# The first four token tiles of a transformer block kernel: two queues for the first load, normalisation on VectorE in column parts, casts in halves, another order of the first matmuls

## The chip, the cores and the metric

The kernel runs on one core of a Trainium2 chip. The metric is device microseconds of one execution; the number given for the kernel before is the median of its runs. A profiled execution, with a record of every instruction, is what the views of the profile are taken from.

## What is computed

`x` is 2048 tokens of 576 values. One block adds local attention and a two-layer Mish network, both on the same normalised tokens:

```python
xn = (x - mean(x)) / sqrt(var(x) + 1e-5)          # over the 576 values of a token
q, k, v = split(xn @ wqkv)                         # 32 heads of 18
# each token attends to itself and to tokens 2, 4, ... 14 before it
o = softmax(q . k * 18**-0.5 over those 8) @ v
h = xn @ w1 + b1                                   # 4608 wide
out = x + o @ wo + (h * tanh(softplus(h))) @ w2
```

All of it is float32. For the matmuls on TensorE (PE) each operand is split into a high and a low part of a shorter type (`fp32r` in the rows): the high part is a cast, the low part the residual, and a product is the sum of high·high, high·low and low·high.

## The kernel before, in words

The tokens are taken in two halves of 1024 (`hf`), each in two blocks of 512 (`b`, TB), each of four tiles of 128 tokens (`jj`, JB). The QKV weights come in four groups of 432 columns (`g`), each of five row blocks of 128 (576 values padded to 640). One item `qkv_item(hf, g, b, jj)` multiplies one token tile by one weight group: 14 matmuls into one PSUM tile `pq`, with a list `seq` of triples (row block of the tokens, row block of the weights, high or low part of the weights). A list `plan` holds the items in an order written out by hand; other work is hung on its slots (`before`, `at`). Each engine takes its instructions in the order of the program, and waits for others by semaphores. DMAs are issued by SP's queue (`nc.sync`) in the program's order.

The first half begins with the items of weight group 0 on tiles 0 to 3, by `first_item(n)` (L1205); then come group 1 on the same tiles and so on. This is the part that the change touches.

- **Start** (L49 to L65): ScalarE (ACT) loads its function table at L49; GpSimd (POOL) builds the identity matrix; 30 transposes of it (L65) keep PE busy until data are there ("warm").
- **Loads** (L1106 to L1113, `load_x` L51): on SP's queue in this order: token tile 0 (`acc_0_0_0`, shown as acc), two row blocks of group 0's weights (`rq0`), token tile 1, the other three row blocks. The function `hold` (L1115) puts the loads of tiles 2 and 3 behind tile 0's statistics, and behind them the weights of group 1 and the rest.
- **Normalisation of a tile**: `ln_stats` on VectorE (DVE; two BATCH_NORM_STATS2 at L112, an aggregate at L113); `ln_root` (variance plus epsilon on DVE, L158; logarithm and exponential on ACT, L159 and L160); `ln_newton` (DVE: one Newton step for the root, L167 to L169, and mean·root with its sign changed, L170); `ln_norm` (ACT: one pass over 576 columns with scale and bias, L180; POOL: a copy of the last 64 columns beside them, L181, so that the fifth row block is full).
- **Transpose and split** (`ln_transpose` L184, `transpose_split` L67): POOL keeps the last columns for later (`rem`, L192); four transposes on PE into the PSUM tile `ta` (L75) and a fifth into `tb` (L76); ACT casts `ta` to the high parts `xt` in one pass of 512 columns (L81), DVE subtracts to the low parts (L82); ACT casts `tb` (L86), DVE subtracts for its upper 64 partitions (L87).
- **Group 0's weights** (`first_cast` L1176): ACT casts each row block to its high part (L1179), POOL subtracts to the low part (L1180). Later groups have their casts on ACT (L254) and their residuals on DVE (L255).
- **Order**: `prologue` (L1183) writes tile 0's chain and the start of tile 1's, with the five weight casts between. In the item of tile n, `mid` (L1208) is put in before matmul number 11, 8 or 4: it transposes tile n + 1 and prepares the tile after that.

In the item of tile 0 to 2, `seq` is: high·high of row blocks 0 to 3, two low weights, the low tokens of row blocks 0 to 3, two low weights, and the two products of the fifth row block. In tile 3's item it goes row block by row block.

Of the kernel before, what the change touches and what calls it, by code (L numbers as in the profile page):

```python
# [8 lines left out]
F32 = mybir.dt.float32  # L9
# [30 lines left out]
def block_kernel(ctx: ExitStack, tc: tile.TileContext, x, wq, wo, w1, b1, w2, mask, out):  # L40
# [7 lines left out]

    nc.scalar.preload_act_table_set("natural_log_exp_and_others")  # L49

    def load_x(hf, blocks=range(NB), jjs=range(JB)):  # L51
        tiles = []
        xv = x[hf * SH:(hf + 1) * SH, :].rearrange("(p j) d -> p j d", j=TJ)
        for b in blocks:
            for jj in jjs:
                t = sb.tile([P, D], F32, tag="acc", bufs=9, name=f"acc_{hf}_{b}_{jj}")
                nc.sync.dma_start(t, xv[:, b * JB + jj, :])
                tiles.append(t)
        return tiles
# [3 lines left out]
    warm = ps.tile([P, 512], F32, tag="h", bufs=4, name="warm")  # L63
    for k in range(30):
        nc.tensor.transpose(warm[:, (k % 4) * P:(k % 4 + 1) * P], ident, ident)  # L65

    def transpose_split(src, dst, col, extra=None, pair=False):  # L67
        n = next(tpn)
        if pair:
            ta, tb = (ps.tile([P, 512], F32, tag="out", bufs=4, name=f"tt{k}_{n}") for k in range(2))  # L70
        else:
            ta = ps.tile([P, 512], F32, tag="h", bufs=4, name=f"ta_{n}")
            tb = ps.tile([P, 512], F32, tag="h", bufs=4, name=f"tb_{n}")
        for k in range(KT):
            nc.tensor.transpose(ta[:, k * P:(k + 1) * P], src[:, k * P:(k + 1) * P], ident)  # L75
# [5 lines left out]
        nc.scalar.copy(hi, tav)  # L81
        nc.vector.tensor_sub(dst[:, 5:5 + KT, col:col + P], tav, hi.bitcast(F32))  # L82
        e = 1 if extra is None else 2
        hr = dst[:, KT:KT + 5 * e - 4:5, col:col + P]
        tbv = tb.rearrange("p (k t) -> p k t", k=KT)[:, 0:e]
        nc.scalar.copy(hr, tbv)  # L86
        nc.vector.tensor_sub(hr[64:P], tbv[64:P], hr[64:P].bitcast(F32))  # L87

# [73 lines left out]
    def ln_newton(n0):  # L162
        g = group[n0]
        k, rs, ve, y, nm = g["k"], *(g[w][:, 0:g["k"]] for w in ("rs", "ve", "y", "nm"))
        if k == 1:
            r, v, y, m = rs[:, 0], ve[:, 0], y[:, 0], nm[:, 0]
            nc.vector.tensor_scalar(y, r, r, v, op0=ALU.mult, op1=ALU.mult)  # L167
            nc.vector.tensor_scalar(y, y, -0.5, 1.5, op0=ALU.mult, op1=ALU.add)
            nc.vector.tensor_scalar(r, r, y, None, op0=ALU.mult)  # L169
            nc.vector.tensor_scalar(m, g["mv"][:, 0, 0:1], r, -1.0, op0=ALU.mult, op1=ALU.mult)  # L170
        else:
# [4 lines left out]
    def ln_norm(n):  # L176
        g = group[n]
        i = n - g["n0"]
        xn = sb.tile([P, 5 * P], F32, tag="xn", bufs=XNB, name=f"xn_0_{n}")
        nc.scalar.activation(xn[:, 0:D], accs[0][n], AF.Identity, bias=g["nm"][:, i, :], scale=g["rs"][:, i, :])  # L180
        nc.gpsimd.tensor_copy(xn[:, D:D + 64], xn[:, KT * P:D])  # L181
        xns[0, n] = xn

    def ln_transpose(hf, b, jj):  # L184
        if jj == 0:
# [7 lines left out]
        else:  # L193
            nc.gpsimd.tensor_tensor(out=rem, in0=rem, in1=xn[:, KT * P:], op=ALU.subtract)
        transpose_split(xn, XTs[hf, b], jj * P, rem if b else None, (hf, b) == (1, 0) and jj < 3)

# [130 lines left out]
    def qkv_item(hf, g, b, jj, mid=None, mid_at=4):  # L327
# [855 lines left out]
    def prologue():  # L1183
# [15 lines left out]
        ln_norm(1)  # L1199
        first_cast(4, nc.gpsimd)()  # L1200
        ln_stats(2)

    def first_item(n):
# [391 lines left out]
```

## Time and profile before

| | |
|---|---|
| Time before | 1114.05 us, median of 3 runs (1113.94 to 1114.44) |
| Profiled execution | 1114.25 us |
| Its span | 1112.5 us, 18203 instructions |
| Granted TensorE clock, mean | 1.00 |
| Busy, share of the span | PE 99%, PE weight load 91%, DVE 76%, POOL 71%, ACT 45% |
| Chain that ended last, by engine | PE 87%, POOL 6%, DVE 3%, issue 2%, ACT 1% |
| DMA | 271.60 MB, mean 244 GB/s |

Times are in microseconds unless marked ns. The span runs from the first to the last recorded instruction. PE is TensorE's matmul side, PEld its weight load, which overlaps PE; DVE, ACT, POOL and SP are VectorE, ScalarE, GpSimd and SyncE, and a name with q behind it (SPq) is that engine's queue. L12 is line 12 of the kernel. A row of the timeline gives start, busy time, engine, line, operation, out<-in, tile size, the count of instructions, and in brackets the idle time before it with what ended it. A row of the chain of waits gives start, length, and who held the chain. A row of the stretches gives the window, its length, then busy time with the count of instructions for PE, PEld, DVE, ACT and POOL, the granted clock, the DMA engines' busy share, and GB/s. A row of a line's instructions gives shortest, median and longest duration in ns, and between which times they ran. In a row of the costliest groups stand busy time and mean ns of one, then the idle time before them and what ended most of it.

### The profile page before, as it was taken

How to read it: one execution, taken by the hardware profiler on the slowest of the kernel's cores; microseconds unless marked ns; L12 is line 12 of the kernel's file. 1: busy time of each engine (PE TensorE's matmuls, PEld its weight loads, DVE VectorE, ACT ScalarE, POOL GpSimd, SP SyncE). 2: the span in 40 equal slices, each digit the busy share in tenths (PEclk: the TensorE clock that was granted, in tenths of full speed). 3: DMA queues.
4: the chain of work that ended last, by engine and by line, in shares of the span. 5: the costliest groups of instructions: out<-in, count | busy, mean ns of one | idle time of the engine just before them, and what ended most of it. 6: DMA issues, size and time to landing. Idle time of an engine off the chain costs nothing.

```text
span 1112.5 us, 18203 instructions
## 1 busy us (share of the span) xinstructions
PE 1101.6 (99%) x6550; PEld 1015.2 (91%) x6550; DVE 849.5 (76%) x1367; ACT 499.5 (45%) x917; POOL 790.8 (71%) x639
## 2 busy tenths in 40 slices
PE   9999999999999999999999999999999999999998
PEld 8999899999999999999999889989989999999998
DVE  6369788888889888897656577786776677777786
ACT  5544655544454544555333354433433344343353
POOL 2479777766679688785788676666688976867532
PEclk9999999999999999999999999999999999999999
DMA  6899696868777758675597898565664657776574
GB/s 202 283 312 316 225 356 214 285 233 276 258 242 264 268 208 301 249 249 204 190 323 241 245 375 307 211 196 196 220 222 170 209 195 223 244 288 219 171 232 142
DMA packets 178270, 271.60 MB, mean 244 GB/s; under 512 B 53218, under 2 KB 120068, under 8 KB 178180
## 3 DMA queue, kind: packets, MB, share of 16 engines
q1 hardware_dynamic: 178180, 270.44, 71.6%
q8 instruction: 52, 0.85, 0.3%
q14 instruction: 38, 0.31, 0.1%
HBM read 160.39 MB, written 110.00 MB: 243 GB/s over the span
## 4 chain that ended last, share of the span: by engine, by line
PE 87%; POOL 6%; DVE 3%; issue 2%; ACT 1%; DMA 0%; SPq 0%; POOLq 0%; DVEq 0%; ACTq 0%
PE h L669 28%; PE po L767 21%; PE pq L348 9%; PE po L880 9%; PE po L859 6%; PE h L675 5%; PE o L1063 5%; PE z L446 3%; POOL pv L571 2%; POOL accP L868 1%; POOL pr L533 1%; POOL act L721 1%; POOL s L620 1%; DMA acc<-in_x 0%; PE ta L75 0%
## 5 line engine op out<-in xcount | busy, mean ns | idle before, releaser
L767 PEld LDWEIGHTS po<-w,act 128*128 128x128 f32 x1728 | 236.4, 188 | 6.0 <-POOL act L721 0.4
L767 PE MATMUL po<-w,act 128*128 128x288 f32 x1728 | 240.7, 295 | 0.1
L533 POOL TENSOR_TENSOR pr<-q,kv 128x576 f32<-128x576 f32 x128 | 196.9, 1563 | 8.5 <-DMA q<-q_d 5.0
L721 POOL TENSOR_TENSOR act<-c,act 128x512 fp32r<-128x512 f32 x81 | 107.3, 1325 | 128.6 <-ACT act L720 128.6
L571 POOL TENSOR_TENSOR pv<-L,kv 128x576 f32<-128x576 f32 x128 | 177.9, 1484 | 26.1 <-DVE L L564 21.2
L771 DVE TENSOR_TENSOR acc<-po,acc 128x288 f32<-128x288 f32 x288 | 119.4, 448 | 29.9 <-PE po L767 29.0
L348 PE MATMUL pq<-wq,xt 128*128 128x432 f32 x672 | 136.5, 361 | 1.0 <-ACT xt L81 1.0
L880 PEld LDWEIGHTS po<-w,act 128*128 128x128 f32 x960 | 130.9, 188 | 4.6 <-DVE accP L883 1.8
L880 PE MATMUL po<-w,act 128*128 128x288 f32 x960 | 133.5, 295 | 1.0 <-DVE accP L883 1.0
L348 PEld LDWEIGHTS pq<-wq,xt 128*128 128x128 f32 x672 | 125.0, 188 | 8.0 <-ACT xt L81 1.8
L715 ACT ACTIVATE c<-c,b1c 128x512 f32<-128x512 f32 x81 | 58.7, 725 | 140.7 <-DVE c L714 140.4
L669 PE MATMUL h<-xt,t 128*128 128x512 f32 x432 | 110.6, 391 | 0.5 <-DVE rt L714 0.3
L669 PE MATMUL h<-S,t 128*128 128x512 f32 x432 | 110.5, 391 | 0.0
L577 DVE TENSOR_REDUCE og<-pv 128x144 f32<-128x1152 f32 x64 | 86.0, 1345 | 25.7 <-POOL pv L571 25.6
L669 PE MATMUL h<-xt,wa 128*128 128x512 f32 x432 | 104.1, 390 | 0.0
L538 DVE TENSOR_REDUCE L<-pr 128x64 f32<-128x1152 f32 x64 | 85.8, 1341 | 23.8 <-POOL pr L533 23.7
L703 ACT COPY c<-h 128x512 f32<-128x512 f32 x81 | 47.4, 586 | 124.1 <-PE h L675 73.0
L859 PEld LDWEIGHTS po<-pw,u 128*128 128x128 f32 x672 | 92.2, 188 | 5.4 <-DVE u L813 2.1
L859 PE MATMUL po<-pw,u 128*128 128x288 f32 x672 | 94.3, 295 | 2.5 <-DVE u L813 1.6
L669 PEld LDWEIGHTS h<-xt,wa 128*128 128x128 f32 x432 | 80.9, 188 | 17.0
L669 PEld LDWEIGHTS h<-xt,t 128*128 128x128 f32 x432 | 79.0, 188 | 15.7 <-DVE rt L714 0.7
L883 DVE TENSOR_TENSOR accP<-po,accP 128x288 f32<-128x288 f32 x160 | 68.9, 452 | 29.8 <-PE po L880 28.2
(228 smaller groups left out, 1853.8 us busy)
## 6 DMA issues: line engine op xcount, KB each, us to landing
kv<-kv_d SPq DMA_DIRECT2D x64, 396.0 KB, 5.1
kept_t<-t SPq DMA_DIRECT2D x36, 512.0 KB, 4.8
t<-kept_t SPq DMA_DIRECT2D x36, 512.0 KB, 6.7
rw<-in_w SPq DMA_DIRECT2D x36, 320.0 KB, 4.4
kept_wa<-wa SPq DMA_DIRECT2D x18, 640.0 KB, 4.7
kept_w<-w SPq DMA_DIRECT2D x20, 576.0 KB, 4.1
wa<-kept_wa SPq DMA_DIRECT2D x18, 640.0 KB, 5.2
w<-kept_w SPq DMA_DIRECT2D x20, 576.0 KB, 4.1
```

What stands on the lines that cost most here:

```text
L348: nc.tensor.matmul(pq[:, 0:432], XT[:, xi, tok], wt[wi][:, hl, 0:432], start=i == 0, stop=i == len(seq) - 1)
L533: nc.gpsimd.tensor_tensor(out=pr[:, x:x + hh], in0=q[:, j0 + x:j0 + x + hh, None, :].to_broadcast([P, hh, W, CU]), in1=win(kt, 0, CU, j0 + ...
L538: nc.vector.tensor_reduce(L[:, k, j0:j0 + hj].rearrange("p j w h -> p (j w h)"), pr.rearrange("p j w (h d) -> p (j w h) d", h=2), axis=AX, ...
L571: nc.gpsimd.tensor_tensor(out=pr[:, x:x + hj].rearrange("p j d w -> p j w d"), in0=L[:, k, x:x + hj, :, h:h + 1].to_broadcast([P, hj, W, DH]),
L577: nc.vector.tensor_reduce(og[:, c0:c0 + DH, :].rearrange("p d j -> p j d"), pr, axis=AX, op=ALU.add)
L669: nc.tensor.matmul(ph, wt[:, wl, wk * P:(wk + 1) * P], X[:, xs, :], start=first and i == 0, stop=last and i == len(seq) - 1, skip_group_ch ...
L721: nc.gpsimd.tensor_tensor(out=a[:, 1, :], in0=t, in1=a[:, 0, :].bitcast(F32), op=ALU.subtract)
L767: nc.tensor.matmul(po, acts[hf, q, b, j][:, al, tok], done["w2", hf, 2 * q + j][:, wl, c * HC:(c + 1) * HC], start=i == 0, stop=i == 5)
L771: nc.vector.tensor_tensor(out=t, in0=po, in1=t, op=ALU.add)
L859: nc.tensor.matmul(po, units[e, k, qq][:, al, tok], w[:, qq, wl, :], start=i == 0, stop=i == 5)
L880: nc.tensor.matmul(po, acts[hf, q, b, j][:, al, tok], done["w2", hf, 2 * q + j][:, wl, c * HC:(c + 1) * HC], start=i == 0, stop=i == 5)
L883: nc.vector.tensor_tensor(out=t, in0=po, in1=t, op=ALU.add)
```

## The change

The edits all lie in the first four token tiles, weight group 0:

- **First load**: tile 0 is loaded in two halves of 64 partitions, one issued by ACT's queue, one by SP's. ACT's function table is loaded behind that issue.
- **Warm-up**: 24 transposes instead of 30.
- **Normalisation** of tiles 0 to 3: DVE computes (x - mean)·root in three parts, columns 0 to 255, 256 to 575, and the last 64 again into the padding. ACT's pass, POOL's copy and the DVE instruction for the bias (L170) go, for these tiles.
- **Casts in halves**: for these tiles ACT casts `ta` in two passes of 256 columns (`apart`). In tile 0 the subtractions come in halves too; `transpose_split` hands the subtractions back as functions, so that the caller places them.
- **Order**: in the prologue the first two weight casts come behind tile 0's Newton step, the third and fourth around tile 1's statistics, the fifth behind tile 1's Newton step. In the items, `mid` comes before matmul number 11, 12 and 12: transposes of tile n + 1, then statistics and root of tile n + 2, then the subtractions of tile n + 1, then Newton and normalisation of tile n + 2. Tile 0's item has a `seq` of its own, written out; tiles 1 and 2 have all four low weights in a row.

In the changed kernel the lines are: load L56 to L59, warm-up L67, transposes L77 and L78, casts of `ta` in halves L90, subtractions L86 and L87 (tile 0: L94 by halves), cast of `tb` L92 (tile 0: L96), normalisation on DVE L194, weights' high and low parts L1198 and L1199, the items' matmuls L366, later weights' residuals L271.

```diff
...
-    nc.scalar.preload_act_table_set("natural_log_exp_and_others")
...
-                nc.sync.dma_start(t, xv[:, b * JB + jj, :])
+                if (hf, b, jj) == (0, 0, 0):
+                    nc.scalar.dma_start(t[64:P], xv[64:P, 0, :])
+                    nc.sync.dma_start(t[0:64], xv[0:64, 0, :])
+                else:
+                    nc.sync.dma_start(t, xv[:, b * JB + jj, :])
...
-    for k in range(30):
+    for k in range(24):
         nc.tensor.transpose(warm[:, (k % 4) * P:(k % 4 + 1) * P], ident, ident)
...
-        nc.scalar.copy(hi, tav)
-        nc.vector.tensor_sub(dst[:, 5:5 + KT, col:col + P], tav, hi.bitcast(F32))
...
+        lows = [lambda: nc.vector.tensor_sub(dst[:, 5:5 + KT, col:col + P], tav, hi.bitcast(F32)),
+                lambda: nc.vector.tensor_sub(hr[64:P], tbv[64:P], hr[64:P].bitcast(F32))]
+        if apart:
+            for k in (0, 2):
+                nc.scalar.copy(hi[:, k:k + 2], tav[:, k:k + 2])
+            if apart > 1:
+                nc.scalar.copy(hr, tbv)
+                return lows
+            return [lambda k=k: nc.vector.tensor_sub(dst[:, 5 + k:7 + k, col:col + P], tav[:, k:k + 2],
+                                                     hi[:, k:k + 2].bitcast(F32)) for k in (0, 2)] + [
+                    lambda: nc.scalar.copy(hr, tbv), lows[1]]
...
-            nc.vector.tensor_scalar(m, g["mv"][:, 0, 0:1], r, -1.0, op0=ALU.mult, op1=ALU.mult)
...
+        if n < JB:
+            for o0, i0, w in ((0, 0, 256), (256, 256, D - 256), (D, KT * P, 64)):
+                nc.vector.tensor_scalar(xn[:, o0:o0 + w], accs[0][n][:, i0:i0 + w], g["mv"][:, 0, 0:1], g["rs"][:, 0, :],
+                                        op0=ALU.subtract, op1=ALU.mult)
+            return
...
         if mid is not None:
-            seq = [(k, k, 0) for k in range(KT)] + [(0, 0, 1), (1, 1, 1)]
-            seq += [(k + 5, k, 0) for k in range(KT)] + [(2, 2, 1), (3, 3, 1)]
+            seq = [(k, k, 0) for k in range(KT)] + [(k, k, 1) for k in range(KT)] + [(k + 5, k, 0) for k in range(KT)]
         seq += [(4, 4, 0), (4, 4, 1)]
+        if (hf, g, b, jj) == (0, 0, 0, 0):
+            seq = [(0, 0, 0), (1, 1, 0), (5, 0, 0), (6, 1, 0), (0, 0, 1), (2, 2, 0), (1, 1, 1), (3, 3, 0), (2, 2, 1),
+                   (7, 2, 0), (8, 3, 0), (3, 3, 1), (4, 4, 0), (4, 4, 1)]
...
     accs = {0: load_x(0, [0], [0])}
+    nc.scalar.preload_act_table_set("natural_log_exp_and_others")
...
         ln_root(0)
-        first_cast(0, nc.gpsimd)()
         ln_newton(0)
+        for k in range(2):
+            first_cast(k, nc.gpsimd)()
+        ln_norm(0)
+        lo0, lo2, high_r, low_r = ln_transpose(0, 0, 0, 1)
+        lo0()
+        first_cast(2, nc.gpsimd)()
         ln_stats(1)
-        low1 = first_cast(1, nc.gpsimd)
-        ln_norm(0)
-        low1()
-        first_cast(2, nc.gpsimd)()
+        first_cast(3, nc.gpsimd)()
         ln_root(1)
+        lo2()
+        high_r()
         ln_newton(1)
-        ln_transpose(0, 0, 0)
-        first_cast(3, nc.gpsimd)()
+        first_cast(4, nc.gpsimd)()
         ln_norm(1)
-        first_cast(4, nc.gpsimd)()
-        ln_stats(2)
+        low_r()
...
         def mid():
-            if n == 0:
-                ln_root(2)
-                ln_newton(2)
-            if n == 1:
-                ln_root(3)
-                ln_newton(3)
-            ln_transpose(0, 0, n + 1)
-            if n == 0:
-                ln_norm(2)
-                ln_stats(3)
-            if n == 1:
-                ln_norm(3)
-        if n < JB - 1:
-            qkv_item(0, 0, 0, n, mid, (11, 8, 4)[n])
-        else:
-            qkv_item(0, 0, 0, n)
+            lows = ln_transpose(0, 0, n + 1, 2)
+            if n < JB - 2:
+                ln_stats(n + 2)
+                ln_root(n + 2)
+            for f in lows:
+                f()
+            if n < JB - 2:
+                ln_newton(n + 2)
+                ln_norm(n + 2)
+        qkv_item(0, 0, 0, n, mid if n < JB - 1 else None, (11, 12, 12, 0)[n])
```

More of the change, by code (lines that the diff above doesn't have):

```diff
@@ L85, in transpose_split @@
         tbv = tb.rearrange("p (k t) -> p k t", k=KT)[:, 0:e]
+        lows = [lambda: nc.vector.tensor_sub(dst[:, 5:5 + KT, col:col + P], tav, hi.bitcast(F32)),
[9 more added lines that the diff above has]
+                    lambda: nc.scalar.copy(hr, tbv), lows[1]]
+        nc.scalar.copy(hi, tav)
+        lows[0]()
         nc.scalar.copy(hr, tbv)
-        nc.vector.tensor_sub(hr[64:P], tbv[64:P], hr[64:P].bitcast(F32))
+        lows[1]()
     XTs = {}
@@ L178, in ln_norm, with ln_transpose @@
         i = n - g["n0"]
-        xn = sb.tile([P, 5 * P], F32, tag="xn", bufs=XNB, name=f"xn_0_{n}")
+        xn = xns[0, n] = sb.tile([P, 5 * P], F32, tag="xn", bufs=XNB, name=f"xn_0_{n}")
+        if n < JB:
[3 more added lines that the diff above has]
+            return
         nc.scalar.activation(xn[:, 0:D], accs[0][n], AF.Identity, bias=g["nm"][:, i, :], scale=g["rs"][:, i, :])
         nc.gpsimd.tensor_copy(xn[:, D:D + 64], xn[:, KT * P:D])
-        xns[0, n] = xn
-    def ln_transpose(hf, b, jj):
+    def ln_transpose(hf, b, jj, apart=0):
         if jj == 0:
@@ L194, in ln_transpose @@
             nc.gpsimd.tensor_tensor(out=rem, in0=rem, in1=xn[:, KT * P:], op=ALU.subtract)
-        transpose_split(xn, XTs[hf, b], jj * P, rem if b else None, (hf, b) == (1, 0) and jj < 3)
+        return transpose_split(xn, XTs[hf, b], jj * P, rem if b else None, (hf, b) == (1, 0) and jj < 3, apart)
     def raw_load(src, width, name):
```

4 lines of the change are left out of this document (2 added, 2 removed).

## The prediction

> **What bounds the kernel now.** I read the page's first part, then busy time by stretches, then the chain of waits over the first 40 us, then the timeline up to 26 us. The page and the stretches:
>
> ```profile
> PE 1101.6 (99%) x6550; PEld 1015.2 (91%) x6550; DVE 849.5 (76%) x1367; ACT 499.5 (45%) x917; POOL 790.8 (71%) x639
> ```
>
> ```profile
> 0.00:9.08 9.08, 6.90 (x35) 6.66 (x35) 4.12 (x15) 4.93 (x11) 3.46 (x10) 1.00 0.77 247
> 9.08:18.03 8.95, 8.37 (x42) 6.63 (x43) 7.33 (x24) 6.22 (x17) 4.02 (x8) 1.00 0.66 245
> 18.03:26.00 7.97, 7.97 (x43) 7.62 (x44) 5.80 (x15) 4.49 (x13) 0.53 (x2) 1.00 0.25 74
> 26.00:100.00 74.00, 74.00 (x388) 70.60 (x387) 44.37 (x59) 32.76 (x91) 50.58 (x42) 1.00 0.87 290
> ```
>
> PE is the bound from 18.03 us on: it is busy without a gap up to 100. Its first 9 us are warm-up, and up to 18.03 it waits for data. So the change is worth what it does to the moment at which PE has the four tiles behind it; PE passes that moment on to the end one for one.
>
> ```profile
> 2.10 4.72 DMA acc<-in_x
> 6.84 0.83 DVE st L112 x2
> 10.51 0.83 DVE st L112 x2
> 14.30 0.83 DVE st L112 x2
> 18.03 0.66 PE ta L75 x4
> 18.80 12.99 PE pq L348 x66
> ```
>
> These are pieces of the chain. Until the fourth tile's transposes at 18.03 it runs over VectorE: one tile's statistics begin 3.67 and then 3.79 us after the other's. The tile period is VectorE's, not PE's: one item is 14 matmuls of 0.197 us (66 in 12.99) and five transposes of about 0.12 (0.47 for four, below), 3.4 us in all. The timeline has the pieces:
>
> ```profile
> 0.72 0.39 SPq L57 DMA_DIRECT2D acc<-in_x  x1
> 1.34 6.12 PEld L65 LDWEIGHTS warm<-ident 128*128 128x128 f32 x30 [1.34 <-POOL ident masks.py:199]
> 3.68 0.82 DVE L112 BATCH_NORM_STATS2 st<-acc 128x6 f32<-128x288 f32 x2 [2.32 <-DMA acc<-in_x]
> 5.43 0.27 DVE L167 TENSOR_SCALAR y<-rs,ve 128x1 f32<-128x1 f32 x1 [0.51 <-ACT rs L160]
> 5.92 1.10 POOL L1180 TENSOR_TENSOR wq<-rq,wq 128x432 fp32r<-128x432 f32 x1 [4.63 <-ACT wq L1179]
> 5.93 0.21 DVE L169 TENSOR_SCALAR rs<-rs,y 128x1 f32<-128x1 f32 x1
> 6.17 0.22 DVE L170 TENSOR_SCALAR nm<-mv,rs 128x1 f32<-128x1 f32 x1
> 6.48 0.87 ACT L180 ACTIVATE xn<-acc,nm,rs 128x576 f32<-128x576 f32 x1 [0.19 <-ACT wq L1179]
> 7.42 0.47 PEld L75 LDWEIGHTS ta<-ident,xn 128*128 128x128 f32 x4
> 7.69 0.21 DVE L113 BATCH_NORM_AGGREGATE mv<-st 128x2 f32<-128x12 f32 x1
> 8.46 0.57 ACT L81 CAST xt<-ta 128x512 fp32r<-128x512 f32 x1
> 9.09 2.47 PE L348 MATMUL pq<-wq,xt 128*128 128x432 f32 x11 [0.84 <-ACT xt L81]
> 9.47 0.68 DVE L82 TENSOR_TENSOR xt<-ta,xt 128x512 fp32r<-128x512 f32 x1
> 10.18 0.29 DVE L87 TENSOR_TENSOR xt<-tb,xt 64x128 fp32r<-64x128 f32 x1
> 11.19 0.56 PEld L75 LDWEIGHTS ta<-ident,xn 128*128 128x128 f32 x4
> 18.55 7.74 PE L348 MATMUL pq<-wq,xt 128*128 128x432 f32 x38
> 18.93 1.13 DVE L255 TENSOR_TENSOR wq<-rwq,wq 128x432 fp32r<-128x432 f32 x2 [0.85 <-ACT wq L254]
> ```
>
> Behind the fourth tile's transposes 24 matmuls of the first weight group remain; from 18.55 they end at about 23.4, where group 1 begins.
>
> **The change, part by part.** All times are in the profiled execution.
>
> First load in halves. Issue to use takes 2.96 us (0.72 to 3.68). The first piece's issue, 0.39 us on SP, is shared with ScalarE. Bounds: 0.5 us earlier (that issue and a little more), 0.4 later (the weights' loads behind it get in between). I take 0.2 earlier. [...] ScalarE's table load now stands behind its DMA issue; ScalarE has nothing else to do until the first statistics, from 3.68, are done, which hides it. SP's next loads, the first weights, are issued no later than before.
>
> Warm-up of 24 instead of 30. At 0.204 us each it ends 1.2 us sooner, near 6.3. It hides behind tile 0's chain as before. If PE's pace (0.204 per warm-up transpose, 0.12 from 7.42 on, though the clock granted in the rows is 1.00 throughout) doubles later for it, matmuls are slower in a stage where VectorE sets the pace; I put 0.3 us on that as the upper end, and 0 in the sum.
>
> Normalisation on VectorE. Per tile, 0.87 us of ScalarE, a POOL copy and the 0.22 of L170 go. The first two lay beside VectorE's residual subtractions (L82, L87), so VectorE's own sum decides. It gains three TENSOR_SCALARs with two per-partition operands, over 256, 320 and 64 columns. The fixed part is that of L167, 0.27. The columns cost 1.0 ns each by L82 against L87 ((0.68 - 0.29) us over 384), or at best half. So the three are 0.41 to 0.54, 0.44 to 0.61 and 0.30 to 0.34; as they follow each other without a wait, some 0.08 of each overlaps (the two L112 of 0.444 take 0.82, row below): 1.0 to 1.3 us per tile.
>
> The tile period then is: statistics 0.82, aggregate 0.21, variance 0.15, the subtractions 0.69 and 0.29 (now beside ScalarE's square root, whose 0.51 us wait goes), Newton 0.27, 0.15, 0.21, the parts 1.0 to 1.3, and some nine gaps of 0.03 (L169's end at 6.14 to L170 at 6.17): 4.1 to 4.4 us instead of 3.7 to 3.8. ScalarE is relieved, but it was not what the tiles waited for.
>
> What stands beside the parts. POOL's residuals of the first weights (L1180, 1.10 us each) run just then. What the trace shows of such neighbours:
>
> ```profile
> 65.72 1.29 POOL L620 TENSOR_TENSOR s_u<-xt 128x512 f32<-128x512 f32 x1 [4.11 <-DMA q_d<-qs]
> 65.81 1.67 DVE L255 TENSOR_TENSOR wq<-rwq,wq 128x432 fp32r<-128x432 f32 x1 [1.54 <-ACT wq L254]
> 67.09 1.55 POOL L620 TENSOR_TENSOR s<-s,s_u 128x512 f32<-128x512 f32 x1
> 67.40 1.34 DVE L538 TENSOR_REDUCE L<-pr 128x64 f32<-128x1152 f32 x1
> ```
>
> ```profile
> L112 DVE BATCH_NORM_STATS2 st<-acc x12: 406/444/461, 3.7 to 24.7; 128x6 f32<-128x288 f32 x12
> ```
>
> ```profile
> L255 DVE TENSOR_TENSOR wq<-rwq,wq x15: 600/610/1830, 18.9 to 77.1; 128x432 fp32r<-128x432 f32 x15
> ```
>
> ```profile
> L593 DVE STREAM_TRANSPOSE oT<-og x16: 759/778/781, 141.0 to 1049.8; 128x576 f32<-128x576 f32 x16
> ```
>
> ```profile
> L167 DVE TENSOR_SCALAR y<-rs,ve 128x1 f32<-128x1 f32 x4 | 1.1, 272 | 2.0 <-ACT rs L160 2.0
> L158 DVE TENSOR_SCALAR ve<-mv 128x1 f32<-128x1 f32 x4 | 0.6, 154 | 0.1
> L158 DVE TENSOR_SCALAR ve<-mv 128x2 f32<-128x2 f32 x2 | 0.3, 170 | 0.1
> ```
>
> An L255, 0.60 us alone, took 1.67: it ended 0.47 after POOL's instruction had, and POOL's next was stretched in its turn. The two engines take turns, an instruction each. TENSOR_REDUCE and STREAM_TRANSPOSE, with one input, are untouched (1.34, and 759 to 781 ns throughout). So the wide TENSOR_SCALAR, which before does not have, costs nothing more by these two rows, and a POOL instruction by L255's. It is nearest to L255 in kind, an elementwise pass from SBUF to SBUF. [...] I take turns with POOL, and the columns at the faster rate. [...]
>
> Casts in halves. One row more:
>
> ```profile
> L911 ACT COPY ot<-o x8: 369/372/377, 1041.7 to 1096.7; 128x256 f32<-128x256 f32 x8
> ```
>
> In the order of the built program, with its waits, both halves of a tile's cast wait for the same count of PE, set by the fourth transpose, and tile 0's first subtraction waits for the second half. So the halves start no earlier; the first ends 0.2 us before the whole would (0.37 for 256 columns by L911, 0.57 for 512 by L81).
>
> The walk, with the first load 0.2 earlier. Tile 0: the root is ready at 5.94 (before: 6.14); part one is issued against POOL's L1180 (5.72 to 6.82) and ends at 7.1; POOL's second L1180 is next, to 8.2; part two ends at 8.4, part three at 8.6. Transposes three and four run at 8.45 and 8.65, the first half's cast from 8.95 to 9.32, PE's first matmul at 9.37 instead of 9.09. VectorE, in order, does the first subtraction (9.63 to 10.06), and only then tile 1's statistics (before: at 6.84); subtraction two ends at 11.7, Newton at 12.6. Tile 1's part one meets POOL's last L1180 (12.5 to 13.6; its cast now stands behind the square root on ScalarE) and ends at 13.9; the transposes start at 13.95 (before: 11.19). Tile 2's statistics: 14.85 (10.51). POOL is free by now. With 4.1 us per tile, the transposes of tile 2 start at 18.35, tile 3's statistics at 18.9, its transposes at 22.45 (18.03). Behind them 16 matmuls remain, not 24. But item 3's third one needs the subtraction, which VectorE does behind part three (ends 23.0) and the two weight residuals of L255 (to 24.3): it ends at 25.0. Then 0.3 and eleven steps of 0.197: group 1 begins at 27.5. The same walk through before's order gives 23.5. So it is 4.0 us later; nothing in PE's 74 gapless us behind it takes that back. The load of group 1's last weights hangs on the first L255 and moves with it, and the weights' share of VectorE moves as a whole, so nothing new is late there.
>
> The new matmul order costs nothing and gains nothing: each has its operands in that order, but VectorE holds up the next tile.
>
> **The rivals.** First, no turns, and columns at half price (1.0 us per tile). The first matmul comes at 8.1; lost is VectorE's wait for tile 0's casts, ahead of tile 1's statistics (8.8 instead of 6.84), and the longer period. Transposes of tile 1 at 11.75, of tile 3 at 20.25, group 1 at 25.3: 1.8 later. For it: the one-input rows.
>
> Second, no turns, and 1.0 ns per column: a period of 4.4 and group 1 at 26.3: 2.8 later. For it: every wide VectorE row here streams at that rate.
>
> Third, the other side: VectorE gets no longer. Place: L194, the three parts. If one part costs up to 0.17 us, the tile period falls to 3.5, PE profits from its first matmul at 8.1, and group 1 begins at 23.35 or, at 0.1 us, 23.1: 0.1 to 0.4 us sooner. It decides at 0.17 per part; against it, L167 takes 0.27 for a single column.
>
> Fourth, the change doesn't load earlier: the halves land late by 0.4 instead of early by 0.2, and PE speeds up late (0.3): forecast plus 0.9, 4.9 later.
>
> **How the numbers follow.** The profiled execution took 1114.25 (span 1112.5 and 1.75 around it); the median is 0.2 below. Forecast 1114.05 + 4.0 = **1118.0** (chance 0.5). No turns, half price: 1115.9 (0.14). No turns, full columns: 1116.9 (0.19). Later still: 1119 (0.07). Other side: 1113.8 (0.1). 0.2% is 2.2 us, about what a measurement of this kernel can tell from no change. Slower by more: the forecast, the later case, and most of the full-column case, 0.74. Within: half price, the rest of that, most of the other side, 0.22. Faster by more: 0.04, a shift that no walk here gives. The range runs from 1114.8, no turns and half price with a fixed part of L158's 0.154 instead of 0.27 (0.35 less per tile, over three tiles), to 1119.3.
>
> **What would show it.** In the changed kernel: L194's 256-column part at 1.1 us or more in tiles 0 and 1 beside L1199, and near 0.4 in tiles 2 and 3 (0.4 everywhere: no turns; 0.54: full columns); the first L366 matmul near 9.4; tile statistics 4.1 us apart at the end; the last tile's transposes near 22.4; group 1 near 27.5. Wrong would be a fourth tile's transpose at or before 18 us, or a period below 3.7.

## The result, and the profile after

The changed kernel takes 1120.08 us (median of 5 runs, 1118.92 to 1120.95); the kernel before, beside it, 1114.44 us (5 runs, 1113.94 to 1114.96). The ratio is 1.005, 95% interval 1.0038 to 1.0061: slower by 4.2 to 6.8 us. The forecast was 1118.0, with a range up to 1119.3.

First the page, then busy time by the same stretches as before (window, length, then PE, PEld, DVE, ACT, POOL, the granted clock, DMA share, GB/s):

```profile
PE 1104.2 (99%) x6544; PEld 1015.3 (91%) x6544; DVE 854.3 (76%) x1376; ACT 496.5 (44%) x917; POOL 790.7 (71%) x635
```

```profile
0.00:9.08 9.08, 5.29 (x27) 4.82 (x28) 4.56 (x11) 2.58 (x5) 2.89 (x8) 0.98 0.77 239
9.08:18.00 8.92, 8.62 (x32) 7.05 (x33) 7.07 (x22) 4.25 (x15) 3.89 (x5) 0.63 0.67 254
18.00:26.00 8.00, 7.15 (x36) 5.13 (x35) 7.57 (x22) 4.80 (x16) 1.42 (x2) 1.00 0.11 28
26.00:100.00 74.00, 74.00 (x389) 70.57 (x388) 41.44 (x66) 32.36 (x89) 45.89 (x39) 1.00 0.83 277
```

From 26 to 100 us PE is again without a gap, so whatever was lost in front of it stays lost. Two things in the first stretches are new: VectorE is busy 7.57 of 8 us from 18 to 26 (before: 5.80 of 7.97), and the granted clock has fallen to 0.63 in the second stretch.

The chain of waits, start, length and holder:

```profile
0.72 3.51 DMA acc<-in_x
...
4.32 0.83 DVE st L125 x2
...
6.82 2.14 DVE xn L194 x2
8.96 0.04 issue
9.01 0.70 PE ta L77 x2
9.73 0.66 ACT xt L90 x2
10.41 0.42 DVE xt L94
10.83 0.74 DVE st L125 x2
...
13.24 1.73 DVE xn L194 x3
...
15.34 0.83 DVE st L125 x2
...
24.45 0.70 DVE xt L86
25.16 0.04 issue
25.20 10.87 PE pq L366 x54
```

Of the 54 matmuls from 25.20 on 12 are the fourth item's (the rest are three items of group 1), so group 1 begins at 25.20 + 12 x 0.201 = 27.6. The record of the fourth item's last matmul is at 27.46, before at 23.17. The next record, one spacing of 0.2 behind, is group 1's first: **27.66 against 23.36, 4.3 us later** (forecast: 27.5, 4.0 later). I use this mark for all kernels below; between executions of one program up to that point it varied by up to 0.3 (the last section shows where that comes from).

The shift is still there at the attention stage (first of its matmuls at 599.53 instead of 595.29). The profiled execution then lost 1.4 more at 692 us, where PE waited for VectorE and that for a load of tokens. Another execution of the same kernel, second row, didn't:

```profile
690.00:700.00 10.00, 8.62 (x54) 7.69 (x53) 8.96 (x13) 5.00 (x11) 5.59 (x5) 1.00 0.81 265
```

```profile
690.00:700.00 10.00, 10.00 (x65) 9.37 (x65) 8.21 (x14) 4.88 (x10) 5.62 (x5) 1.00 0.76 262
```

### The profile page after: what moved, and what is told of

The parts are those of the page before. It is cut to its first block, busy times and chain, and to the rows that moved or that the text cites. A ratio compares the mean times of both kernels' runs of the same rounds, so it can differ in the third digit from the quotient of the medians.

```text
span 1118.9 us, 18201 instructions
## 1 busy us (share of the span) xinstructions
PE 1104.2 (99%) x6544; PEld 1015.3 (91%) x6544; DVE 854.3 (76%) x1376; ACT 496.5 (44%) x917; POOL 790.7 (71%) x635
## 4 chain that ended last, share of the span: by engine, by line
PE 87%; DVE 4%; POOL 3%; DMA 3%; ACT 1%; issue 1%; SPq 0%; DVEq 0%; POOLq 0%; ACTq 0%
PE h L687 28%; PE po L785 20%; PE po L898 10%; PE pq L366 9%; PE po L877 6%; PE h L693 5%; PE o L1081 4%; PE z L464 3%; POOL pv L589 1%; DMA t<-kept_t 1%; POOL s L638 1%; DMA accP<-in_x 1%; DMA o<-o_d 1%; PE ta L77 0%; POOL act L739 0%
## 5 line engine op out<-in xcount | busy, mean ns | idle before, releaser
L366 PE MATMUL pq<-wq,xt 128*128 128x432 f32 x672 | 138.2, 364 | 0.7 <-DVE xt L86 0.4
L366 PEld LDWEIGHTS pq<-wq,xt 128*128 128x128 f32 x672 | 126.5, 190 | 8.0 <-ACT xt L90 1.2
L556 DVE TENSOR_REDUCE L<-pr 128x64 f32<-128x1152 f32 x64 | 85.8, 1341 | 25.2 <-POOL pr L551 25.1
```

The source lines that it names most:

```text
L366: nc.tensor.matmul(pq[:, 0:432], XT[:, xi, tok], wt[wi][:, hl, 0:432], start=i == 0, stop=i == len(seq) - 1)
L556: nc.vector.tensor_reduce(L[:, k, j0:j0 + hj].rearrange("p j w h -> p (j w h)"), pr.rearrange("p j w (h d) -> p (j w h) d", h=2), axis=AX, ...
```

## The experiments

All marks in one table. "Rest" is the span less the start of group 1, worked out from one profiled execution of each kernel; e6 to e11 have that execution only, so their marks carry the argument and not their times. In e4 and e14 the mark stands behind the 40 added transposes.

| kernel | first statistics | 4th tile's transposes | group 1 | rest | time (runs) |
|---|---|---|---|---|---|
| before | 3.68 | 18.03 | 23.4 | 1089.1 | 1114.44 (5) |
| changed | 4.32 | 22.95 | 27.7 | 1091.2 | 1120.08 (5) |
| e1 split load only | 4.36 | 18.80 | 24.2 | 1090.2 | 1115.99 (10) |
| e2 normalisation only | 3.69 | 22.42 | 27.8 | 1090.9 | 1119.73 (4) |
| e3 changed, ScalarE normalises | 4.36 | 22.69 | 27.9 | 1089.1 | 1118.97 (6) |
| e4 delay only | 3.69 | 17.76 | 27.4 | 1089.2 | 1118.61 (5) |
| e5 changed again | 4.38 | 23.00 | 27.7 | 1089.5 | 1119.52 (4) |
| e6 no first low parts | 4.29 | 20.57 | 25.3 | 1089.5 | 1116.52 (1) |
| e7 statistics first | 4.24 | 22.33 | 27.0 | 1089.7 | 1118.46 (1) |
| e8 Newton last | 3.70 | 19.73 | 25.1 | 1089.3 | 1116.19 (1) |
| e9 one queue | 3.72 | 22.10 | 26.8 | 1089.4 | 1118.33 (1) |
| e10 warm-up 30 | 4.32 | 22.72 | 27.4 | 1089.6 | 1118.79 (1) |
| e11 lows behind | 4.46 | 22.12 | 26.8 | 1089.6 | 1118.18 (1) |
| e12 mended | 3.76 | 21.15 | 25.9 | 1091.7 | 1117.18 (10) |
| e13 changed, five rounds | 4.26 | 22.88 | 27.6 | 1089.5 | 1121.72 (5) |
| e14 delay, five rounds | 3.68 | 17.84 | 27.5 | 1090.7 | 1119.95 (5) |

**e1, the split load (and the table load behind it) in the kernel before**

```diff
+                if (hf, b, jj) == (0, 0, 0):
+                    nc.scalar.dma_start(t[64:P], xv[64:P, 0, :])
+                    nc.sync.dma_start(t[0:64], xv[0:64, 0, :])
+                else:
+                    nc.sync.dma_start(t, xv[:, b * JB + jj, :])
...
+    nc.scalar.preload_act_table_set("natural_log_exp_and_others")
```

> The kernel before with the first load alone in halves on two queues (and ScalarE's table load behind that issue). In the changed kernel the first statistics began at 4.32 us instead of 3.68. If the two-queue load is what made that, statistics begin near 4.3 here too, the fourth tile's transposes and group 1 come at most 0.64 later (group 1 at 23.5 to 24.0), and the time is +0.1 to +0.65. If the load was late for another reason (the warm-up, the table load), statistics begin near 3.7 and the time is within 0.1 of before. If a second queue disturbs the loads of the later stages, the time is more than 1 us over, with the shift at group 1 no larger than 0.65.

Statistics began at 4.36 and group 1 at 24.2, 0.8 later (0.64 at most was expected; the excess is within the mark's scatter). So the late load comes with the split and not with the shorter warm-up or the order. ScalarE's table load moves with it, from 0.71 to 1.31, here and back in e9; no run moves one without the other, so its share isn't shown. The time stands at a ratio of 1.0008 (0.9998 to 1.0017) to before, which alone would not tell it from no change; the marks do. The issues of e1, size and time from issue to landing:

```profile
acc<-in_x ACTq DMA_DIRECT2D x1, 144.0 KB, 2.9
acc<-in_x SPq DMA_DIRECT2D x1, 144.0 KB, 3.5
```

Both were issued at 0.72. A half takes as long as the whole did on one queue (0.72 to 3.65), and the second half 0.6 longer. In the packet records of e1 the ACT half's run from 2.06 to 2.92 and the SP half's from 2.61 to 3.35 (when they begin, 38 of the other 64 have begun and 23 are through); the whole's ran from 1.74 to 3.28. So the packets begin later and end only 0.08 later; most of the loss lies between the last packet and the landing, 0.9 for the SP half against 0.4 for the whole. Why that grows, the records don't show. The issues themselves grow too, in the timeline of the changed kernel to 0.56 and 0.60 from 0.39:

```profile
0.72 0.56 ACTq L56 DMA_DIRECT2D acc<-in_x  x1
...
0.72 0.60 SPq L57 DMA_DIRECT2D acc<-in_x  x1
```

The packets of both halves end no sooner than the whole's (3.35 against 3.28), though they overlap from 2.61 to 2.92, and the first statistics begin 0.68 us later in e1 (4.36 against 3.68) and 0.64 in the changed kernel (4.32).

**e2, normalisation on VectorE alone; e3, all of the change but that.** e2 is the kernel before with the new branch in `ln_norm` (and without L170); e3 is the changed kernel without them:

```diff
-        if n < JB:
-            for o0, i0, w in ((0, 0, 256), (256, 256, D - 256), (D, KT * P, 64)):
-                nc.vector.tensor_scalar(xn[:, o0:o0 + w], accs[0][n][:, i0:i0 + w], g["mv"][:, 0, 0:1], g["rs"][:, 0, :],
-                                        op0=ALU.subtract, op1=ALU.mult)
-            return
...
+            nc.vector.tensor_scalar(m, g["mv"][:, 0, 0:1], r, -1.0, op0=ALU.mult, op1=ALU.mult)
```

> The kernel before with the first four tiles normalised by VectorE in column parts, nothing else changed. If VectorE's parts with the turns against GpSimd are the cost, the 256-column part takes near 1.0 us in tiles 0 and 1 (it is in their neighbourhood that GpSimd works on the first weights) and group 1 comes 3.5 to 5 us later (27 to 28.5), the time +3.5 to +5. If the order of the work is the cost and the normalisation is not, group 1 comes less than 1.5 us later and the time is below +1.5.

> The changed kernel with the normalisation of the first four tiles given back to ScalarE (and GpSimd's copy); load, warm-up, halves and order as changed. If the normalisation on VectorE is the cost, group 1 comes within 1.2 us of before's 23.4 (the late load 0.64, the rest the order) and the time is below +1.5. If the order costs as much by itself, because VectorE now waits for tile 0's casts ahead of tile 1's statistics and ScalarE's pass stands behind its casts, group 1 comes 3 to 4.3 us later (26.4 to 27.7) and the time is +3 to +5.5.

Each by itself costs what both cost together: group 1 at 27.8 and 27.9 against 27.7. So neither is "the" cause; giving one back leaves the other's limit, which lies at nearly the same place. In e3 the 4.6 us are the load's 0.7 and 1.9 more up to tile 1's transposes (both together 13.92 instead of 11.39; VectorE waits for tile 0's casts ahead of tile 1's statistics), then 2.1 from there to the fourth tile's (8.8 us instead of 6.6). The limits are different ones. In the stretches 16 to 20 and 20 to 24, the changed kernel first, then e3, VectorE (third busy time) is full in the one and not in the other:

```profile
16.00:20.00 4.00, 3.76 (x21) 2.97 (x20) 3.73 (x13) 1.64 (x9) 0.29 (x1) 1.00 0.00 0
20.00:24.00 4.00, 3.81 (x21) 2.94 (x19) 3.73 (x13) 2.62 (x11) 0.55 (x1) 1.00 0.00 0
```

```profile
16.00:20.00 4.00, 3.37 (x19) 2.62 (x18) 2.56 (x10) 2.30 (x8) 0.53 (x2) 1.00 0.00 0
20.00:24.00 4.00, 3.20 (x18) 2.41 (x16) 1.93 (x7) 2.37 (x7) 0.53 (x2) 1.00 0.02 4
```

What limits e3, whose tiles still come 4.4 us apart with no engine full, stands in its own chain from the transposes at 18.30 to the next at 22.69:

```profile
18.30 0.67 PE ta L77 x4
...
19.68 0.70 DVE xt L86
...
21.77 0.87 ACT xn L193
```

Between these rows lie the two casts (19.00) and the Newton step (20.73): each waits for the one before it. e8 shows which edit makes it.

**e8, one step moved in the kernel before**

```diff
             if n == 0:
                 ln_root(2)
-                ln_newton(2)
             if n == 1:
                 ln_root(3)
-                ln_newton(3)
             ln_transpose(0, 0, n + 1)
+            if n == 0:
+                ln_newton(2)
+            if n == 1:
+                ln_newton(3)
             if n == 0:
                 ln_norm(2)
```

> The kernel before with one move: in the first two items the Newton step of tile n + 2 is written behind the transposes, casts and subtractions of tile n + 1, as in the changed kernel; ScalarE normalises, first load and prologue as before. If the place of that step is what made the changed order slow even with ScalarE's normalisation (each tile then waits for the last one's transposes, casts and subtractions, one after the other), tiles 2 and 3 come 1 us or more later each, and group 1 at 25 to 26 instead of 23.4. If the order's cost comes from the prologue alone (tile 1's statistics behind tile 0's casts), group 1 is within 0.4 of 23.4.

Group 1 came at 25.1, 1.7 later, tiles 2 and 3 4.3 us apart. Its timeline from tile 1's transposes to tile 2's:

```profile
11.10 0.60 PE L75 MATMUL ta<-ident,xn 128*128 128x128 f32 x4
11.79 0.57 ACT L81 CAST xt<-ta 128x512 fp32r<-128x512 f32 x1
12.39 0.69 DVE L82 TENSOR_TENSOR xt<-ta,xt 128x512 fp32r<-128x512 f32 x1 [0.98 <-ACT xt L81]
13.11 0.29 DVE L87 TENSOR_TENSOR xt<-tb,xt 64x128 fp32r<-64x128 f32 x1
13.44 0.27 DVE L167 TENSOR_SCALAR y<-rs,ve 128x1 f32<-128x1 f32 x1
14.48 0.87 ACT L180 ACTIVATE xn<-acc,nm,rs 128x576 f32<-128x576 f32 x1 [1.96 <-issue]
15.40 0.66 PE L75 MATMUL ta<-ident,xn 128*128 128x128 f32 x4 [0.93 <-ACT xn L180]
```

The next tile's Newton step, ready since its square root, stands in VectorE's queue behind a subtraction that waits for this tile's cast (0.98 idle). That closes a ring: transposes, cast, subtractions, Newton, normalisation, next transposes, one after the other, 4.3 us (11.10 to 15.40). In the order before, Newton (12.27) and statistics run ahead of the subtraction (13.26) and the ring is open. The ring alone costs 1.7 here and, by the marks above, 2.1 of e3's 4.6.

**e6 and e11, the turns with GpSimd.** e6 leaves out the low parts of group 0's weights (GpSimd writes zeros); e11 keeps them and puts the first two behind tile 0's normalised columns:

```diff
-        return lambda: eng.tensor_tensor(out=t[:, 1, :], in0=rq0[k], in1=t[:, 0, :].bitcast(F32),
-                                         op=ALU.subtract)
+        return lambda: eng.memset(t[:, 1, :].bitcast(F32), 0.0)
```

```diff
-        for k in range(2):
-            first_cast(k, nc.gpsimd)()
+        lows01 = [first_cast(k, nc.gpsimd) for k in range(2)]
         ln_norm(0)
         lo0, lo2, high_r, low_r = ln_transpose(0, 0, 0, 1)
+        for f in lows01:
+            f()
```

> The changed kernel with the low parts of the first five weight blocks left out: GpSimd fills them with zero (a short instruction without an input) in place of its 1.1 us subtractions, so the product with those low parts is missing. If the turns with GpSimd are what the first two tiles lose, L194's first two parts take near 0.42 in all tiles, tile 0's three parts 1.0 instead of 2.35, tile 1's 1.0 instead of 1.73, and group 1 comes 1.5 to 2.6 sooner than in the changed kernel (25.1 to 26.2). If the turns are hidden behind the casts and the order, group 1 moves by less than 0.7. What is left over before's 23.4 then belongs to the order and the late load.

> The changed kernel with GpSimd's first two subtractions placed behind its copy for tile 0's remainder, so that they wait for tile 0's normalised columns. Tile 0's three parts then have no GpSimd beside them. With turns as the cost, they take 1.0 instead of 2.35 and tile 0's transposes come 1.0 to 1.3 sooner; group 1 gains less, 0.6 to 1.2, as the weights' low parts come later and a turn falls into tile 1 or its neighbours. If group 1 stays within 0.3 of 27.7, tile 0's turns were hidden by what follows them.

The three parts of L194, tiles 0 to 3, in the timeline of the changed kernel (with GpSimd's row beside tile 0) and of e6:

```profile
6.57 2.20 POOL L1199 TENSOR_TENSOR wq<-rq,wq 128x432 fp32r<-128x432 f32 x2 [5.28 <-ACT wq L1198]
...
6.82 2.35 DVE L194 TENSOR_SCALAR xn<-acc,mv,rs 128x256 f32<-128x256 f32 x3
...
13.24 1.73 DVE L194 TENSOR_SCALAR xn<-acc,mv,rs 128x256 f32<-128x256 f32 x3
...
18.42 0.99 DVE L194 TENSOR_SCALAR xn<-acc,mv,rs 128x256 f32<-128x256 f32 x3
...
22.39 0.99 DVE L194 TENSOR_SCALAR xn<-acc,mv,rs 128x256 f32<-128x256 f32 x3
```

```profile
6.79 0.99 DVE L194 TENSOR_SCALAR xn<-acc,mv,rs 128x256 f32<-128x256 f32 x3
11.60 0.99 DVE L194 TENSOR_SCALAR xn<-acc,mv,rs 128x256 f32<-128x256 f32 x3
16.04 0.99 DVE L194 TENSOR_SCALAR xn<-acc,mv,rs 128x256 f32<-128x256 f32 x3
20.01 0.99 DVE L194 TENSOR_SCALAR xn<-acc,mv,rs 128x256 f32<-128x256 f32 x3
```

2.35 and 1.73 where GpSimd subtracts (beside tile 1 until 14.25), 0.99 where it doesn't (e6's short fills fall beside none of the parts). With the subtractions gone, group 1 is 2.4 sooner; the stretched parts themselves add up to 2.1. The groups by form, tile 0 of the changed kernel, then tile 2 (busy, mean ns):

```profile
L194 DVE TENSOR_SCALAR xn<-acc,mv,rs 128x320 f32<-128x320 f32 x1 | 1.2, 1218 | 0.0
L194 DVE TENSOR_SCALAR xn<-acc,mv,rs 128x256 f32<-128x256 f32 x1 | 1.0, 986 | 0.0
```

```profile
L194 DVE TENSOR_SCALAR xn<-acc,mv,rs 128x320 f32<-128x320 f32 x1 | 0.4, 440 | 0.0
L194 DVE TENSOR_SCALAR xn<-acc,mv,rs 128x256 f32<-128x256 f32 x1 | 0.4, 412 | 0.0
L194 DVE TENSOR_SCALAR xn<-acc,mv,rs 128x64 f32<-128x64 f32 x1 | 0.3, 306 | 0.0
```

From 64 to 256 columns it is 106 ns, 0.55 per column, and a fixed part of 0.27. In e11 tile 0's parts took 0.99, and tile 1's 2.36 instead of 1.73: part of the turns moved to the next tile, and group 1 gained 0.8 of the 1.4.

**e7, e9, e10, e12: the remaining parts, each in the changed kernel.** e7 puts tile 1's statistics ahead of tile 0's first subtraction; e9 loads tile 0 whole on SP's queue and loads ScalarE's table at the start; e10 has 30 warm-up transposes; e12 has these three and e11's move.

```diff
+        ln_stats(1)
         lo0()
         first_cast(2, nc.gpsimd)()
-        ln_stats(1)
```

```diff
-                if (hf, b, jj) == (0, 0, 0):
-                    nc.scalar.dma_start(t[64:P], xv[64:P, 0, :])
-                    nc.sync.dma_start(t[0:64], xv[0:64, 0, :])
-                else:
-                    nc.sync.dma_start(t, xv[:, b * JB + jj, :])
+                nc.sync.dma_start(t, xv[:, b * JB + jj, :])
```

```diff
-    for k in range(24):
+    for k in range(30):
```

> The changed kernel with tile 1's statistics ahead of tile 0's first subtraction on VectorE. VectorE idled 1.24 us there, waiting for the second half's cast. If that wait is on the path, tile 1's statistics begin near 9.2 instead of 10.75 and its transposes and group 1 come 0.4 to 1.2 sooner (26.4 to 27.3). If VectorE's order there is of no account, because the turn with GpSimd or PE sets tile 1, group 1 is within 0.3 of 27.66.

> The changed kernel with the first load whole on SP's queue and ScalarE's table load at the start again; nothing else undone. The split alone put the first statistics from 3.69 to 4.36 and group 1 from 23.4 to 24.15. If that loss is carried through the changed start as well, statistics begin near 3.7 and group 1 at 26.9 to 27.2 instead of 27.7. If GpSimd's turns or the casts hold the first tile anyway, group 1 moves by less than 0.3.

> The changed kernel with 30 warm-up transposes instead of 24. Of the runs so far those with 24 show a granted clock of 0.50 from about 9 to 15 us, those with 30 show 1.00. If the shorter warm-up is the reason, the clock stays at 1.00 here, item 0's matmuls come 0.2 us apart instead of 0.36 to 0.4. If TensorE's half clock costs time, group 1 is 0.5 or more sooner (27.2 or less); if VectorE sets the pace there, group 1 is 0 to 0.4 sooner. If the clock falls here too, the cause is PE's idle time at 6 to 9 us and not the number of transposes.

> The changed kernel with four places undone or mended at once: first load whole on one queue, 30 warm-up transposes, GpSimd's first two subtractions behind tile 0's normalisation, and tile 1's statistics ahead of tile 0's first subtraction. If these terms add up (0.6 to 0.8, 0 to 0.4, 0.6 to 1.2, 0.65), group 1 comes at 24.6 to 25.8 and the time is +1.2 to +2.5 over before; what stays is VectorE's period of 3.98 us against 3.5. If they hide behind one another, group 1 is at 26 or later and the time above +2.6. Faster than before it is by neither.

e7 gained 0.6 (tile 1's statistics at 9.06): about half of VectorE's 1.24 us of waiting for tile 0's casts was on the path. e9 gained 0.9: the load's loss goes through. e10 gained 0.2, within the scatter of the mark, and its clock fell, against what its expectation put first. The granted clock from 10 to 15 us (third figure from the end) in the changed kernel, in e9 with 24 transposes, and in e10 with 30:

```profile
10.00:15.00 5.00, 4.79 (x14) 3.79 (x14) 4.22 (x12) 2.29 (x8) 3.31 (x3) 0.50 1.00 377
```

```profile
10.00:15.00 5.00, 3.46 (x17) 2.62 (x18) 4.59 (x14) 2.02 (x8) 3.61 (x4) 1.00 0.93 347
```

```profile
10.00:15.00 5.00, 4.70 (x17) 3.57 (x17) 4.45 (x13) 2.05 (x7) 3.50 (x4) 0.66 1.01 382
```

The number of transposes alone doesn't decide it: with 24 the clock stayed at 1.00 in e9 and e11, with 30 it fell in e10 (what goes with the fall stands in the last section). PE's idle time, the cause that its expectation names for this case, is not shown to be it either: PE was busy for 1.94 of the 3.41 us ahead of e10's fall, and for only 1.71 in e9, where the clock stayed. The fall costs little here: e9 gained without the fall about what the load alone had lost in e1 (0.9 against 0.8).

e12 came to 25.9, 1.8 sooner than the changed kernel; the four single gains add up to 2.6, so 0.8 of them hide behind one another. Its time is 1.002 of before (1.0011 to 1.003), 2.5 us over by marks and medians: at the edge between the two cases of the expectation, so the terms neither add up whole nor all hide. In its timeline GpSimd's five subtractions follow each other, and all turns fall into tile 1:

```profile
6.26 0.99 DVE L192 TENSOR_SCALAR xn<-acc,mv,rs 128x256 f32<-128x256 f32 x3
...
10.23 2.94 DVE L192 TENSOR_SCALAR xn<-acc,mv,rs 128x256 f32<-128x256 f32 x3
```

```profile
7.57 5.55 POOL L1196 TENSOR_TENSOR wq<-rq,wq 128x432 fp32r<-128x432 f32 x5
```

No arrangement tried here is faster than the kernel before.

**e4, e5, e13, e14: what lies behind group 1.** e5 and e13 are the changed kernel again; e4 and e14 are the kernel before with a bare delay of PE:

```diff
+        if (hf, g, b, jj) == (0, 1, 0, 0):
+            for _ in range(40):
+                nc.tensor.transpose(pq[:, 0:P], ident, ident)
```

> The kernel before with 40 more transposes of the identity (about 4.3 us of TensorE) ahead of group 1's first matmul, nothing else changed. If PE passes a later start on one for one and no more, the time is +4.2 to +4.6, and its spread is that of before. If a shift of this size by itself brings the stall of 1.4 us that the changed kernel shows at 692 us (behind loads of tokens for the accumulators), the time is +5 to +6.5 and PE shows that gap. If PE's 74 gapless us hide part of a shift, it is below +4.

> The changed kernel once more, for its spread. Group 1 begins 4.3 us later than before (27.66 against 23.36); its first five runs were 1118.92 to 1120.95. In the delay-only kernel a shift of the same size gave no stall at 692 us. If the 1.3 us beyond the shift are chance (loads that come late in some executions of any of these kernels), the new runs reach down to 1118.5 or lower, the profile may or may not show the gap at 692, and the difference of the lowest runs is 4.0 to 4.9. If they belong to the change, the gap is there again and no run is below 1118.9.

> The changed kernel in five rounds beside the bare delay. If what lies beyond the start's 4.3 and the end's 0.3 is chance, its lowest and its median are 0.3 to 0.9 over those of the bare delay, and its median is 4.4 to 5.2 over before. If the change makes later stalls more frequent, its median is more than 1.2 over the bare delay's, with the lowest still 0.3 to 0.9 over.

> The kernel before with 40 transposes (4.36 us of TensorE) ahead of group 1, in five rounds. PE passes the delay on one for one: median and lowest 4.0 to 4.6 over those of before. If a shifted kernel meets its later loads worse, its median is more than 5 over before with the lowest still near 4.2.

The delay is passed on: e4's ratio is 1.0037 (1.0024 to 1.005), 4.1 us, with group 1 4.0 later and the rest as before (4.2 to 4.6 was expected). The changed kernel without the stall at 692 (e5, e13) has a rest of 1089.5; the other kernels with VectorE's normalisation and the changed order have 1089.4 to 1089.7 where no stall shows, so 0.3 to 0.6 more. In e5 and e13 0.3 of it lies behind 1053 us, in the last products; why it goes with this change was not tried.

The rest is single executions. Over all sessions the lowest and the median are 1113.94 and 1114.7 for before (50 executions), 1118.80 and 1120.05 for the changed kernel (14), 1118.25 and 1119.25 for the bare delay (10). More than 1.2 us over its own lowest are 11 of 50, 8 of 14 and 4 of 10. Where a profile caught one, PE waited late in the second half: 1.38 at 692 in the changed kernel, 2.41 instead of 0.8 at 820 in e12 and e14, 0.70 at 688 in e1; e2's profile lost 1.6 behind its last matmul. In e13 and e14 the accounts that left the stalls to chance failed, and both others came out by their numbers: the changed kernel's median is 1.8 over the bare delay's with its lowest 0.55 over ("more frequent"), and the bare delay's own is 5.2 over before with its lowest 4.1 over ("a shift meets its loads worse"). So these stalls come with a bare shift too; whether the change adds to their number, five executions of each don't settle, and it stays open.

## Why the prediction went wrong

The direction, and the place and size of the start's loss, were right; the time came out 2.1 above the forecast and 0.8 above the range. By its own steps:

- **What bounds the kernel**: held. PE passes group 1's start on one for one (e4: 4.0 us at group 1, 4.1 in the time).
- **First load in halves**: the step that failed in sign. 0.2 earlier was forecast, with 0.4 later as the bound; it was 0.64 later, and e1 and e9 put 0.8 and 0.9 on it at group 1. The bound reckoned with loads behind the split, not with longer issues (0.56 and 0.60 instead of 0.39), later first packets (2.06 instead of 1.74) and a landing 0.9 instead of 0.4 behind the last packet. The table load, which the prediction took to be hidden, moved along, and its share isn't shown.
- **Turns with GpSimd**: right, and the largest term: 2.4 us by e6. The sum with full columns fell (0.55 ns per column), and so did the one without turns. That a column costs at best half of 1.0 ns was the author's estimate, which no row of before shows; the 0.55 of the changed kernel stands in its place. Of its signs, the 256-column part took 1.15 in tile 1, but 0.99 in tile 0, short of the 1.1 that was named.
- **Casts in halves**: right; both halves ran back to back behind the fourth transpose (9.73), and VectorE's wait for them cost 0.6 (e7).
- **Tile period**: 4.1 forecast, 3.98 measured (statistics at 15.34 and 19.32). From the first statistics to group 1 the walk had 24.0 us, the chip took 23.3; half of the difference lies ahead of tile 2's statistics (11.4 against 11.0), half behind the last transposes (5.05 against 4.71). That overestimate of 0.7 hid most of the load's error of 0.84: that group 1 came out at 27.66 against 27.5 is luck in part, two errors of opposite sign.
- **"ScalarE is relieved, but it was not what the tiles waited for", and order at no cost**: true of the kernel before, wrong as an account of the change. With ScalarE's normalisation the rest of the change makes group 1 as late (e3, 27.9), 2.1 of it by the ring that e8 shows. The forecast had terms for the normalisation and for VectorE's wait for tile 0's casts, and none for the ring.
- **Warm-up**: no cost from its number, as forecast. That the clock falls to half a little later was not foreseen; by e9 and e10 it cost no more than the mark's scatter of 0.3.
- **"Nothing new is late there", and the range with it**: the step that put the time outside. Everything behind group 1's start was put at nothing, and the range's upper end held only mechanisms of the first 27 us. Measured were 0.4 behind group 1 even without a stall, and stalls of 1 to 4 us in single executions, which put the changed kernel's median 1.2 over its lowest (before: 0.5). The 2.0 us by which the time passed 1114.05 + 4.0 are, as an estimate from these numbers, 0.3 from the start, 0.4 from this rest, 0.4 because the kernel before itself took 1114.44 beside it and not 1114.05, and the remaining 0.9 from the stalls. That the rest grows is shown; why, stays open.

## What to carry to other kernels

Moving work to the engine that sets the pace is paid in full here (e2: group 1 at 27.8 instead of 23.4), and the price of an elementwise pass there depended on who ran beside it (three parts 0.99 us alone, 2.35 and 1.73 beside GpSimd's subtractions): look which GpSimd instructions fall into the same microseconds before counting 0.4 us for it. When steps are reordered, follow each ring through the in-order queues (who waits behind the waiting instruction), since a new order and a new engine can each set the same pace, and undoing one then shows nothing. A range needs a term for what single executions do far behind the change, taken from the spread of the kernel before.

## What was not expected of the hardware

- A load of 288 KB split over two queues (with ScalarE's table load behind one of the issues) landed 0.6 us later than whole: 2.9 and 3.5 us from issue to landing for the halves (e1), 2.9 for the whole (before).
- In the changed kernel's profile TensorE's granted clock stayed at 1.00 for 3.41 us from 5.37 on, at 0.50 for 6.83, then at 1.00 for 1102.5: 1, 2 and 323 times 3.413. At the start it fell to 0.50 for one such step in e3, e6, e7 and e10, for two in all three profiles of the changed kernel, and stayed at 1.00 in e2, e9 and e11. The step ahead of the fall, in the changed kernel, and a step of e2 behind which the clock stayed (second figure: its length, third: PE's busy time):

```profile
5.37:8.78 3.41, 1.19 (x9) 0.71 (x7) 2.77 (x7) 1.30 (x4) 2.20 (x2) 1.00 1.02 360
```

```profile
8.40:11.81 3.41, 2.03 (x11) 1.43 (x12) 2.79 (x8) 1.95 (x6) 1.59 (x3) 1.00 1.05 382
```

  In the step ahead of the fall PE was busy for 1.16 us of 3.41 in e3, 1.19 in the changed kernel, 1.22 in e7, 1.25 in e5, 1.47 in e13, 1.91 in e6 and 1.94 in e10. In the first step at full clock of profiles where the clock then stayed, it was busy for 1.71 in e2 and e9, 1.73 in e11, 2.13 in e14, 2.56 in before and 2.84 in e12. So less work of PE goes with the fall, but between 1.71 and 1.94 the two groups overlap, and what decides there these traces don't show. In the changed kernel's two steps at 0.50 PE was busy for 2.94, with another such step behind it, and 3.36, with full clock behind it. Where the first step at full clock begins varies by execution: at 5.37, 4.39 and 4.82 us in the three profiles of the changed kernel.
- Ahead of its first step at full clock a trace has no record of the clock (before: up to 7.24 us, changed kernel: up to 5.37), and the views show 1.00 there. But in both the warm-up transposes come 0.213 us apart up to that step and 0.109 behind it, so the start runs at half pace; the prediction's 1.00 "throughout" was read from rows without a record. In before, e14 and e4, one program up to the mark, that step begins at 7.24, 5.51 and 4.95 and the fourth item is through at 23.36, 23.18 and 23.09: the scatter of the mark goes with it.
- VectorE's TENSOR_SCALAR parts took longer beside GpSimd's TENSOR_TENSOR: in the changed kernel 412 ns (tile 2) became 986 in tile 0, and 440 became 1218, while GpSimd's two instructions took 1.10 and 1.15 us, 1.11 on average in before. The two parts ended at 7.81 and 8.95, 0.14 and 0.18 us behind the ends of GpSimd's instructions (7.67, 8.77), which is what turns of one instruction each would give. In e6, where zeros are filled in instead, tile 0's parts took 414 and 442.
